# Nine of the twenty chunk states computed on ScalarE in eight pieces, two half differences on GpSimd, sums and products merged, and a new order of the whole program

## The chip, the cores and the metric

The kernel runs on one core of a Trainium2 chip. The metric is the device time of one execution in microseconds, lower is better. The core has five instruction streams that run side by side, each in its own fixed order, and wait for each other through semaphores: TensorE (PE), VectorE (DVE), ScalarE (ACT), GpSimd (POOL), and SyncE (SP), which here only issues DMAs.

## The reference

Two stages, one after the other. The first is a linear attention with a decaying state, for 4 batches, 8 heads, 768 steps and 48 channels per head; the second is a gated long convolution over 768 steps, with 384 channels.

```
# stage 1, for each batch, head, step t
y[t]  = r[t] @ (state + outer(u*k[t], v[t]))
state = w[t][:, None] * state + outer(k[t], v[t])
# stage 2, x = y with the heads side by side: [4, 768, 384]
x1, x2, x3 = split(x @ w_proj, 3)
conv = irfft(rfft(x2, axis=1) * rfft(filter, axis=0), axis=1)
out  = (x1 * conv * x3) @ w_out
```

## The kernel before

**Stage 1 by chunks.** The 768 steps of a batch are 6 chunks of 128 steps, so there are 24 chunks, numbered 0 to 23 (chunk c belongs to batch c // 6). For a chunk, SP loads w, k, r and v (`ldw`, `ldk`, `ldr`, `ldv`, line 464, 192 KB each, into rings of six tiles). ACT takes the logarithm of w (`lw`, L470). PE sums it over the steps by triangular masks (`cs`, L474, and `ce`, L480 to L486). ACT takes exponentials (`en`, `eq`, or in place in PSUM as `enp`, `eqp`). DVE or POOL multiplies them with k and r (`kh`, `khp`, `q`, `qp`). PE transposes the two products (`tqk`, L561), and a copy brings them to SBUF (`tT`, the tile qkT, on ACT by L237). PE multiplies them to 8 score matrices of 128x128 (`sc`, L574) in one PSUM tile that is two banks wide, of which there is one only. DVE masks them into SBUF (`mt`, L581). PE then makes the chunk's output y from scores and v and from the queries and the state before the chunk (`y`, L622 and L627; `yb` also adds the bonus term by a matmul with vc, L619; otherwise `xn` on DVE adds it, L639). `xc` copies an output with the bonus in it to SBUF.

**The state.** `kv` (L600, L602) adds to the old state the chunk's outer products in PSUM, 128x384; `S` (L610) scales that by the chunk's whole decay `ph`, which differs by partition and by group of 48 columns: four pairs of heads, two heads each. It is one DVE instruction in which the eight decays of a partition are spread over 48 columns each. The next chunk's `kv` and `y` read the result. The last chunk of a batch has no state, so there are 20.

**The bonus.** `rk` is r times k (POOL L535), `rku` is that times u, `cc` its sum over the channels (DVE L541), `vc` is v times that sum (POOL L555).

**Stage 2 by batches.** Each output is transposed (`yt`, `xT`); the projections `p1`, `p3` (L688) make x1 and x3, which become the gate `g`; sums and differences of the two halves of a batch in time (`sa`, `sb`, `fp`, `fm`) go through the projection `x2` (L719), and cosine and sine matrices F give the spectrum `f` (L734, L739). DVE multiplies it by the filter's spectrum T (`da`, `db`, L761, L764), `pp` adds the two products (L767), `i1` and `i2` transform back (L773), `s` and `d` are their sum and difference, `yy` multiplies by the gate (L807), `po` (L852) projects out, `o` copies, `st` stores. Batch 3, the last, does the way back in halves of the time (`i1h`, `i2h`, `ech`, `sh`, `dh`, `yyh`, `poa`, `pob`).

**The filter.** At the start ACT makes F by a sine (`sin`, L346 to L351, with two loads of its function tables beside the one of `tLn`, L342). The filter is loaded by one DMA of 1152 KB (`ldfilt`, L360); `fs` and `fd` (DVE L399, L402) make the sum and the difference of its halves, `hf` (PE L409, L416) transforms them, and `ht` (ACT L434, a copy from PSUM scaled by a column of the tile rot) and `hr` (DVE L439) turn the result into T.

**The order.** The program is one string, ORDER, of words like `A:ht0.1` or `P:hf0@2`: engine, operation, arguments, PSUM bank. `emit` issues the words one by one, so each engine's words, read in turn, are its queue. There is no scheduler at run time: an instruction that waits holds up all behind it on its engine. A POOL word that ends in `!` also waits for the last DVE instruction of certain kinds ahead of it in the string.

Of the kernel before, what the change touches and what calls it, by code (L numbers as in the profile page):

```python
# [10 lines left out]
FP32 = mybir.dt.float32  # L11
BF16 = mybir.dt.bfloat16
# [30 lines left out]
A:ht0.1 A:mc2 A:ht0.0 S:ldv1 A:enp2 P:hf1@3 P:tqk0@5 V:mem6 V:ms0 A:tT0 P:kv0@0 V:hr0.1 V:ms2
V:hr0.0 V:S0 P:hf2@2 V:khp2 P:sc0@8 A:he P:cs3@0 A:ht1.1 S:ldk3 S:ldw4 P:tqk2@1 A:ht1.0 V:rku2
G:vc0! G:v1! P:ce3@3 P:hf3@5 S:ldr3 S:ldv2 V:mt0 V:cc2 V:hr1.1 P:yb0@2 A:eq3 P:sc1@8 V:hr1.0 G:vc1!
S:ldw5 A:enp3 A:lw4 S:ldv3 V:mt1 A:tT2 A:v2 A:xc0 G:rk3! G:rku3! P:kv1@3 P:hf4@4 P:cs4@5 G:vc2! V:S1
V:khp3 A:enp4 A:ht2.0 P:yb1@1 P:yt0@2 G:v3! G:q3! P:kv2@3 S:ldk4 S:ldr4 V:cc3 S:ldr5 A:lw5 A:ht2.1
S:ldk5 G:rk4! G:vc3! P:ce4@0 P:sc2@8 P:ce5@4 A:xT0 A:xc1 A:eq5 V:S2 S:ldv4 P:hf5@3 P:tqk3@2 A:eqp4
# [904 lines left out]
```

## Time and profile before

| what | value |
|---|---|
| three timed runs | 150.94, 151.19, 152.24 us; median 151.19 |
| the profiled execution | 150.74 us, of which the span from first to last instruction is 148.9 |
| busy, of the span | PE 134.0, DVE 134.8, ACT 130.7, POOL 108.8 us |
| DMA | 27.40 MB, 184 GB/s on the mean |
| stretches, from the view by windows | 0 to 20 us: DVE busy 12.4, ACT 15.5; 20 to 130 us: DVE 109.2, ACT 104.6; 130 to 149 us: DVE 13.2, ACT 10.7 |

Busy time counts an engine as busy from the start of an instruction to its end, and two instructions in a row overlap: the next one begins before the last one has ended. What an instruction costs in a full queue is therefore the time from its start to the next one's start, called its **step** below. It is read from the view in order of time, whose first two columns are the start and the duration.

### The profile page before, as it was taken

To read this page: it belongs to the slowest core of one execution; us is meant where nothing else is said; L and a number is where in the kernel's file an instruction comes from. 1 tells how busy PE (TensorE), PEld (TensorE's weight loads), DVE (VectorE), ACT (ScalarE), POOL (GpSimd) and SP (SyncE) were. 2 spreads that over 40 slices of the span, in tenths; PEclk is the share of its full clock that TensorE was granted. 3 is DMA by queue.
4 is the path that set the end of the run, shared out by engine and by line. 5 is a ranking of instruction groups with operands and counts; after the bars stand their busy time and mean duration, and the time that the engine had idled before them with its cause. 6 is when DMAs were issued, how large, how long until landed. Compare 5 with 4: busy or idle time off the path is not lost.

```text
span 148.9 us, 4080 instructions
## 1 busy us (share of the span) xinstructions
PE 134.0 (90%) x1499; PEld 89.9 (60%) x1499; DVE 134.8 (91%) x278; ACT 130.7 (88%) x274; POOL 108.8 (73%) x133
## 2 busy tenths in 40 slices
PE   6625699898999899999999999999999999999990
PEld 6423365666655567777666757666666776555840
DVE  6534999999999999999999999999999999999950
ACT  3799699999999899999999999999999975768470
POOL 7034179995579799999659999695599995846530
PEclk9955559999999999999999999999999999999998
DMA  4998999999999999989999999989980046001854
GB/s 80 212 278 218 181 210 187 219 188 243 178 258 201 263 203 183 217 167 214 227 232 200 222 204 194 198 168 219 229 186 0 4 173 254 0 0 53 314 210 170
DMA packets 105702, 27.40 MB, mean 184 GB/s; under 512 B 100305, under 2 KB 105682, under 8 KB 105682
## 3 DMA queue, kind: packets, MB, share of 16 engines
q1 hardware_dynamic: 105682, 27.14, 81.1%
q8 instruction: 11, 0.18, 0.5%
q14 instruction: 9, 0.07, 0.1%
HBM read 22.41 MB, written 4.72 MB: 182 GB/s over the span
## 4 chain that ended last, share of the span: by engine, by line
PE 68%; DMA 12%; SPq 5%; POOL 4%; DVE 4%; issue 3%; ACT 1%; ACTq 0%; DVEq 0%; POOLq 0%
PE p L688 14%; PE po L852 8%; PE i L773 6%; PE x L719 6%; PE tqk L561 6%; DMA filt<-in_moe_filter_fft_dram 5%; SPq L464 5%; PE sc L574 4%; DMA ldv<-in_v_dram 4%; DMA ldk<-in_k_dram 3%; PE f L739 3%; PE y L627 2%; PE yt L650 2%; PE cs L474 2%; PE kv L602 2%
## 5 line engine op out<-in xcount | busy, mean ns | idle before, releaser
L535 POOL TENSOR_TENSOR rk<-ldr,ldk 128x384 bf16<-128x384 f32 x23 | 23.0, 1003 | 11.1 <-DMA ldr<-in_r_dram 5.6
L688 PE MATMUL p<-xT,wproj 128*128 128x384 bf16 x144 | 28.8, 326 | 0.0
L555 POOL TENSOR_TENSOR vc<-v,cc 128x384 bf16<-128x384 bf16 x24 | 19.9, 831 | 10.5 <-PE sc L574 3.1
L581 DVE TENSOR_TENSOR mt<-sc,mask_excl 128x1024 bf16<-128x1024 f32 x21 | 25.4, 1210 | 0.1
L237 ACT ACTIVATE qkT<-tqk 128x1024 bf16<-128x1024 bf16 x22 | 22.7, 1031 | 0.7 <-PE tqk L561 0.5
L532 POOL TENSOR_TENSOR qk<-ldr,eq 128x384 bf16<-128x384 f32 x20 | 20.1, 1007 | 3.3 <-DVE rku L538 1.8
L561 PE MATMUL tqk<-ident,qk 128*128 128x128 bf16 x192 | 16.2, 228 | 2.6 <-POOL qk L532 1.8
L688 PEld LDWEIGHTS <-wproj 128*128 128x128 bf16 x144 | 13.0, 97 | 7.4 <-ACT wproj L237 0.3
L561 PEld LDWEIGHTS <-qk 128*128 128x128 bf16 x192 | 12.7, 102 | 5.5 <-POOL qk L532 2.2
L470 ACT ACTIVATE lg<-ldw 128x384 bf16<-128x384 f32 x24 | 12.6, 532 | 2.8 <-DMA ldw<-in_w_dram 2.8
L852 PE MATMUL po<-wout,y 128*128 128x384 bf16 x72 | 14.4, 326 | 0.0
L237 ACT ACTIVATE x<-p 128x384 bf16<-128x384 f32 x24 | 11.7, 505 | 1.5 <-PE p L688 1.5
L237 ACT ACTIVATE ab<-x 128x384 bf16<-128x384 f32 x24 | 11.7, 501 | 1.1 <-PE x L719 0.8
L538 POOL TENSOR_TENSOR rku<-rk,u_bc 128x384 bf16<-128x384 bf16 x13 | 11.8, 913 | 0.4
L541 DVE TENSOR_REDUCE cc<-rku 128x8 f32<-128x384 bf16 x22 | 11.7, 537 | 0.0
L499 ACT ACTIVATE eq<-ce 128x392 f32<-128x392 f32 (+1 forms) x21 | 10.6, 514 | 0.6 <-PE ce L486 0.3
L764 DVE TENSOR_TENSOR UB<-f,T 128x768 bf16<-128x768 f32 x12 | 11.1, 943 | 0.0
L237 ACT ACTIVATE v<-ldv 128x384 bf16<-128x384 f32 x20 | 10.8, 548 | 0.3 <-DMA ldv<-in_v_dram 0.2
L237 ACT ACTIVATE xT<-yt 128x384 bf16<-128x384 bf16 x22 | 10.8, 503 | 0.2
L610 DVE TENSOR_TENSOR S<-kv,eq 128x384 bf16<-128x384 f32 x20 | 10.9, 543 | 0.0
L528 POOL TENSOR_TENSOR qk<-ldk,en 128x384 bf16<-128x384 f32 x10 | 10.0, 1003 | 0.8 <-DMA ldk<-in_k_dram 0.8
L761 DVE TENSOR_TENSOR UA<-f,T 128x768 bf16<-128x768 f32 x11 | 10.3, 943 | 0.1
(152 smaller groups left out, 372.9 us busy)
## 6 DMA issues: line engine op xcount, KB each, us to landing
ldw<-in_w_dram SPq DMA_DIRECT2D x24, 192.0 KB, 3.8
ldr<-in_r_dram SPq DMA_DIRECT2D x24, 192.0 KB, 4.2
ldk<-in_k_dram SPq DMA_DIRECT2D x24, 192.0 KB, 3.7
ldv<-in_v_dram SPq DMA_DIRECT2D x24, 192.0 KB, 3.8
out_dram<-o SPq DMA_DIRECT2D x12, 192.0 KB, 2.3
out_dram<-filt SPq DMA_DIRECT2D x12, 192.0 KB, 2.2
o<-in_moe_w_proj_dram SPq DMA_DIRECT2D x3, 576.0 KB, 6.0
filt<-in_moe_filter_fft_dram SPq DMA_DIRECT2D x1, 1152.0 KB, 8.0
```

The lines of the kernel that those rows point to most:

```text
L237: return nc.scalar.activation(out=o, in_=i, func=AF.Copy)
L470: nc.scalar.activation(out=lg_b[c % 3][:, :, 0:D], in_=ld["w"][c % LD], func=AF.Ln)
L532: return two(e).tensor_mul(qk_b[c % 3][:, 0, :, 0:D], ld["r"][c % LD], eq)
L535: return two(e).tensor_mul(rk_b[c % 2], ld["r"][c % LD], ld["k"][c % LD])
L538: return two(e).tensor_mul(rku_b[c % 2], rk_b[c % 2], u_bc)
L541: nc.vector.tensor_reduce(out=cc_b[c % 3], in_=rku_b[c % 2], axis=AX.X, op=ALU.add)
L555: return two(e).tensor_mul(vc_b[c % 3], v_b[c % 4], cc_b[c % 3].to_broadcast([L, H, D]))
L561: nc.tensor.transpose(p[:, x, j, :], qk_b[c % 3][:, x, 2 * j:2 * j + 2, :], ident)
L581: nc.vector.tensor_mul(mt_b[c % 3], bank_of[f"sc{c}"].rearrange("p q j t -> p (q j) t"), dataclasses.replace(m[:, :], ap=[m[:, :].ap[0], [ ...
L688: nc.tensor.matmul(p, wproj[:, n, cb, fb * L:(fb + 1) * L], xT_b[b % 2][:, NT * hf:NT * hf + NT, cb, :], start=(cb == 0), stop=(cb == CB - 1),
L764: nc.vector.tensor_mul(UB[:, n], twice(bank_of[f"f.{b}.{2 * n + 1}"][:, :]), t2(n, 1))
L852: nc.tensor.matmul(p, y_b[0][:, cb, ti * L:(ti + 1) * L], wout[:, cb, :], start=(cb == FIRST[0]), stop=(cb == FIRST[-1]),)
```

## The change

**States on ACT.** The states of chunks 0, 1, 4, 6, 8, 9, 10, 21 and 22 move from DVE to ACT. ACT can scale by one column of decays per instruction, so each state becomes eight instructions of 128x48.

**GpSimd.** In batch 3, two of the six half differences are made by POOL (`dgh`) from SBUF copies that ACT makes of both sides (`ich` beside `ech`); before, DVE read one side from PSUM. `fd` goes from DVE to POOL.

**Merged.** The products `yy` of a batch's three channel blocks become one instruction of 128x2304 for batches 0 to 2 (`yym`), the sums `pp` become one for batches 0, 1 and 3 (`ppm`), and `fp`, `fm` become one for both parities (`fpm`, and `fmm` for batches 0 to 2). The tiles sd, fo and SD become one tile each for that.

**Counts that shift.** On ACT: 9 states (72 instructions) more, copies `v` 20 to 15, `xc` 15 to 10, `xT` 22 to 19, `wc` 3 to 2, spectrum copies `X` 1 to 5, gate copies `gc` 6 to 8, one table load fewer. On DVE: states 20 to 11, `xn` 9 to 14, `cc` 22 to 24, products from PSUM `da` and `db` 23 to 19. On POOL: `q` 20 to 17, `rku` 13 to 10, `pp` 3 to 1, `v` 4 to 9. On PE: `yb` 15 to 10.

**The order.** All of ORDER is written anew. Two places in it follow.

SP's queue from its start (the tiles' numbers tell the chunk: ldw_79 is chunk 0, ldw_80 chunk 1, ldw_82 chunk 3). Before:

```order
L464 DMA ldw_80<-in_w_dram 128x8x48
L357 DMA u_row<-in_u_dram 1x384
L464 DMA ldw_79<-in_w_dram 128x8x48
L464 DMA ldr_91<-in_r_dram 128x8x48
L464 DMA ldk_85<-in_k_dram 128x8x48
L464 DMA ldk_86<-in_k_dram 128x8x48
L464 DMA ldw_81<-in_w_dram 128x8x48
L464 DMA ldr_92<-in_r_dram 128x8x48
L360 DMA filt<-in_moe_filter_fft_dram 128x6x384
L464 DMA ldv_97<-in_v_dram 128x8x48
L464 DMA ldw_82<-in_w_dram 128x8x48
```

and in the change:

```order
L487 DMA ldw_80<-in_w_dram 128x8x48
L487 DMA ldk_85<-in_k_dram 128x8x48
L487 DMA ldw_79<-in_w_dram 128x8x48
L487 DMA ldv_97<-in_v_dram 128x8x48
L487 DMA ldr_91<-in_r_dram 128x8x48
L487 DMA ldk_86<-in_k_dram 128x8x48
L487 DMA ldr_92<-in_r_dram 128x8x48
L487 DMA ldr_93<-in_r_dram 128x8x48
L383 DMA filt<-in_moe_filter_fft_dram 128x6x384
L487 DMA ldk_88<-in_k_dram 128x8x48
L487 DMA ldw_82<-in_w_dram 128x8x48
```

Ahead of these rows stand ldk_87, ldw_81 and u_row. The filter had seven loads of 192 KB ahead of it and now has ten; ldw_82, chunk 3's w, had nine and the filter, and now has twelve and the filter.

ACT's queue around the first copy of the filter's transform (`E<-hf,rot`, the word ht0.1). Before:

```order
L499 ACTIVATE eq_114<-ce_337 128x392
L237 ACTIVATE m_b<-mtr_318 128x2x192
L237 ACTIVATE v_121<-ldv_97 128x384
L470 ACTIVATE lg_103<-ldw_82 128x8x48
L434 ACTIVATE E_160<-hf_352,rot 128x384
L237 ACTIVATE m_b<-mtr_346 128x2x192
L434 ACTIVATE E_159<-hf_352,rot 128x384
```

and in the change, with the first state behind it:

```order
L522 ACTIVATE eq_113<-ce_334 128x392
L529 ACTIVATE cs_359<-cs_359 128x384
L493 ACTIVATE lg_103<-ldw_82 128x8x48
L457 ACTIVATE E_158<-hf_381,rot 128x384
L457 ACTIVATE E_157<-hf_381,rot 128x384
L240 ACTIVATE qkT_133<-tqk_361 128x1024
L648 ACTIVATE S_137<-kv_370,eq_112 128x48 x8
L533 ACTIVATE ce_404<-ce_404 128x384
```

In both, the first copy stands right behind the logarithm of chunk 3's w (`lg_103<-ldw_82`); in the change less of ACT's other work stands ahead of the two. The state of chunk 0 is eight instructions, each of which scales by one column of the tile eq.

The diff, without most of ORDER and without the renaming of tiles:

```diff
 ORDER = """
-V:mem1 V:mem3 G:mkd! G:mke! G:iota! V:mem0 A:tLn G:mki! S:ldw1 S:ldu S:ldw0 A:lw1 V:mem4 V:mem2
+A:tS0 S:ldk2 S:ldw2 G:iota0! G:mki! G:mkd! G:hm0! V:mem7 V:mem5 G:mke! S:ldu S:ldw1 S:ldk0 S:ldw0
...
     def op_S(e, c):
         ph = eq_b[c % 3][:, C:].rearrange("p (a b) -> p a b", b=2)
+        if e == "A":
+            for j in range(HP):
+                for i in (0, 1):
+                    nc.scalar.activation(
+                        out=S_b[nth(c)][:, j, i], in_=bank_of[f"kv{c}"][:, j, i], func=AF.Copy,
+                        scale=ph[:, j, i:i + 1],
+                    )
+            return
         nc.vector.tensor_mul(
             S_b[nth(c)], bank_of[f"kv{c}"], ph.to_broadcast([L, HP, 2, D])
         )
...
+    def op_fpm(e, b):
+        return two(e).tensor_add(fo[:, :, 0], sd[:, :, 0], sd[:, :, 2])
+
+    def op_fmm(e, b):
+        return two(e).tensor_sub(fo[:, :, 1], sd[:, :, 0], sd[:, :, 2])
...
+    def op_ppm(e, b):
+        return two(e).tensor_add(P_b[b % 2], UA, UB)
+
...
+    def op_ich(e, b, cb, a):
+        copy(e, I_b[cb][:, QUART * a:QUART * a + QUART], bank_of[f"i1h.{b}.{cb}.{a}"][:, 0:QUART])
+
...
+    def op_dgh(e, b, cb, a):
+        sl = slice(QUART * a, QUART * a + QUART)
+        return nc.gpsimd.tensor_sub(back(SD[:, cb, :], a, 1), I_b[cb][:, sl], E_b[cb][:, sl])
+
...
+    def op_yym(e, b):
+        return two(e).tensor_mul(y_b[0], SD, g_b[b % 2])
```

More of the change, by code (lines that the diff above doesn't have):

```diff
@@ L43 @@
[L43 to L48, printed above, removed]
@@ new lines @@
+G:v1! G:vc0! P:cs3@0 A:eqp3 V:mem6 G:v2! P:mtr2@4 A:ms2 S:ldr3 P:hf2@1 G:rk3! S:ldw5 S:ldv3 S:ldk4
+V:mc2 P:tqk1@2 A:en3 A:lw4 V:hb0 V:rku3 V:he A:ht1.1 A:tT1 S:ldr4 P:hf3@4 P:yb0@0 A:ht1.0 A:ph3
+G:kh3! V:cc3 P:kv1@2 G:v3! P:cs4@5 V:qp3 G:vc1! A:lw5 S:ldv4 S:ldw6 S:ldr5 S:ldw8 A:en4 A:S1 P:ce4@1
+V:hr1.1 A:xc0 G:kh4! A:eq4 S:ldk5 P:sc1@8 A:hb1 G:q4! V:mt1 P:tqk3@3 A:tT3 P:hf4@5 V:hr1.0 P:sc2@8
+P:yt0@1 P:kv2@0 P:cs5@4 G:vc3! G:vc2! P:yb1@2 P:ce5@3 A:enp5 A:lw6 A:eqp5 A:xc1 V:mt2 V:S2 P:sc3@8
+P:tqk4@0 V:mt3 P:y3@2 V:qp5 G:rk4! A:tT4 V:khp5 A:ht2.0 P:kv3@0 A:xT0 A:lw8 P:yb2@3 S:ldv5 S:ldk6
@@ new lines @@
+P:po1.4@5 P:p33.1.0@4 P:p13.1.0@3 G:pp2.2! P:sc23@8 P:kv22@1 P:y21@2 A:gc3.1.0 A:gc3.2.0 P:f2.0@0
+V:cc23 V:cc22 A:x13.1.0 V:mt23 A:v23 V:xn21 V:da2.0 P:po1.3@3 G:vc23! A:S22 P:po1.0@4 P:y23@2
+P:p13.2.0@1 P:yt21@0 A:o1.0 A:o1.4 V:xn23 A:x13.2.0 P:p13.0.0@4 G:vc22! P:y22@2 V:pp2.0 P:yt23@1
+A:x13.0.0 A:xT21 V:pp2.1 V:gm2.2.1 G:sb21! A:o1.3 V:xn22 V:sa23 V:sa21 V:sb23 P:i22.2@5 P:i22.1@4
+P:yt22@3 V:sb22 A:ec2.2 V:fpm3 V:fm3.0 P:i12.1@2 P:i22.0@5 A:xT22 P:x23.1.1@0 P:i12.0@3 A:ec2.1
+A:ec2.0 P:i12.2@4 P:x23.1.0@5 V:xT23 V:fm3.1 V:d2.1 V:gm2.1.1 V:d2.0 V:d2.2 A:ab3.1.1 V:s2.1
@@ new lines @@
+A:ab3.1.0 P:x23.0.2@0 P:x23.1.2@1 G:sa22! A:ab3.0.2 P:x23.0.1@5 A:ab3.0.1 A:ab3.1.2 P:p13.2.1@0
+S:st1.4 P:x23.0.0@2 A:ab3.0.0 V:s2.2 P:p13.1.1@5 G:gm3.2.0! P:f3.5@1 P:f3.0@2 V:gm3.1.0 V:s2.0
+A:x13.1.1 A:X3.0 A:X3.5 A:x13.2.1 P:f3.1@3 P:f3.2@5 P:f3.3@2 V:gm2.0.1 V:yym2 P:p13.0.1@1 P:f3.4@0
+G:ua3.0! P:po2.1@4 V:db3.0 V:da3.1 V:ub3.2 P:po2.3@5 P:po2.4@3 A:X3.4 S:st1.3 A:X3.3 S:st0.1 S:st1.2
+S:st0.4 S:st1.1 V:ua3.2 V:ub3.1 A:o2.4 A:o2.3 A:o2.1 A:x13.0.1 P:p33.2.1@2 P:po2.0@0 P:po2.2@3
+V:ppm3 P:p33.1.1@5 S:st0.0 V:g3.1.1 A:gc3.2.1 P:i2h3.0.0@1 A:o2.2 P:i2h3.1.0@4 V:gm3.2.1
@@ L177 @@
     xT_b = ring("xT", 2, [L, NCH, CB, L], BF16)
-    sd_b = ring("sd", 2, [L, NT, CB, L], BF16)
+    sd = consts.tile([L, 2, NT, CB, L], BF16)
     x1_b = ring("x1", 1, [L, CB, S], BF16)
     g_b = ring("g", 2, [L, CB, S], BF16)
-    fo_b = ring("fo", 2, [L, 2, CB, L], BF16)
+    fo = consts.tile([L, 2, 2, CB, L], BF16)
     ab_b = ring("ab", 1, [L, 2, NT, C], BF16)
@@ L187 @@
     E_b = ring("E", 3, [L, HALF], FP32)
-    SD_b = ring("SD", 3, [L, S], BF16)
+    I_b = ring("I", 3, [L, HALF], FP32)
+    SD = consts.tile([L, CB, S], BF16)
     y_b = ring("y", 1, [L, CB, S], BF16)
@@ L194 @@
     u_bc = consts.tile([L, H, D], BF16)
+    hm = consts.tile([L, CB, H], BF16)
+    uh = consts.tile([L, CB, H], BF16)
     filt = consts.tile([L, NCH, C], FP32)
@@ L325, in op_uv, with op_hm, op_um, op_uw @@
         copy(e, u_bc.rearrange("p h d -> p (h d)"), bank_of["us"])
+    def op_hm(e, k_):
+        nc.gpsimd.memset(hm, 1.0)
+        for lo, m in ((0, 1), (D - 1, -1)):
+            nc.gpsimd.affine_select(
+                out=hm, in_=hm, pattern=[[m * L, CB], [-m * D, H]], base=lo,
+                channel_multiplier=m, compare_op=ALU.is_ge, fill=0.0,
+            )
+    def op_um(e, k_, bank):
+        p = ps("um", bank, (L, CB, H))
+        for cb in range(CB):
+            nc.tensor.matmul(
+                p[:, cb, :], u_top[:, cb * L:(cb + 1) * L], mask_incl[:, 0:H],
+                start=True, stop=True,
+            )
+    def op_uw(e, k_):
+        nc.vector.tensor_mul(uh, bank_of["um"], hm)
     def op_ang(e, ti):
@@ L333, in op_ang, with op_tS, op_sn, op_sr @@
             )
-    def op_angn(e, k_):
-        d = ang.rearrange("p (n s) -> p n s", s=S)[:, :, HALF]
         two(e).tensor_scalar(
-            out=d, in0=tcol, scalar1=float(HALF), scalar2=0.5 * UNIT, op0=ALU.mult, op1=ALU.add,
-        )
+            out=ang[:, ti * S + HALF:ti * S + HALF + 1], in0=tcol[:, ti:ti + 1],
+            scalar1=float(HALF), scalar2=0.5 * UNIT, op0=ALU.mult, op1=ALU.add,
+        )
+    def op_tS(e, k_):
+        nc.scalar.preload_act_table(AF.Sin)
     def op_tLn(e, k_):
         nc.scalar.preload_act_table_set("natural_log_exp_and_others")
-    def op_sin(e, k_):
-        for ti in range(NT):
-            nc.scalar.activation(
-                out=F[:, ti, :], in_=low[:, ti * S:(ti + 1) * S], func=AF.Sin,
-                scale=TWO_PI / UNIT,
-            )
+    def op_sn(e, ti):
+        nc.scalar.activation(
+            out=F[:, ti, :], in_=low[:, ti * S:(ti + 1) * S], func=AF.Sin,
+            scale=TWO_PI / UNIT,
+        )
+    def op_sr(e, k_):
         nc.scalar.activation(out=rot, in_=rang, func=AF.Sin, scale=TWO_PI / (2 * S))
-        nc.scalar.preload_act_table_set("natural_log_exp_and_others")
     def op_rsc(e, k_):
@@ L541, in op_cc, with op_rt, op_rT, op_cu @@
         nc.vector.tensor_reduce(out=cc_b[c % 3], in_=rku_b[c % 2], axis=AX.X, op=ALU.add)
-    def op_rh(e, c):
-        x = rku_b[c % 2]
-        return two(e).tensor_add(rh_b[c % 2], x[:, :, 0:D // 2], x[:, :, D // 2:])
-    def op_ch(e, c):
-        nc.vector.tensor_reduce(out=cc_b[c % 3], in_=rh_b[c % 2], axis=AX.X, op=ALU.add)
+    def op_rt(e, c, bank):
+        p = ps(f"rt{c}", bank, (L, CB, L), BF16)
+        f = rk_b[c % 2].rearrange("p h d -> p (h d)")
+        for cb in range(CB):
+            nc.tensor.transpose(p[:, cb, :], f[:, cb * L:(cb + 1) * L], ident)
+    def op_rT(e, c):
+        copy(e, rT_b[c % 2], bank_of[f"rt{c}"])
+    def op_cu(e, c, bank):
+        p = ps(f"cu{c}", bank, (L, H))
+        for cb in range(CB):
+            nc.tensor.matmul(
+                p, rT_b[c % 2][:, cb, :], uh[:, cb, :], start=(cb == 0), stop=(cb == CB - 1)
+            )
+    def op_cv(e, c):
+        copy(e, cc_b[c % 3], bank_of[f"cu{c}"])
     def op_v(e, c):
@@ L645, in op_xc, with op_xr, op_xg @@
         copy(e, xn_b[c % 3], bank_of[f"y{c}"].rearrange("p h d -> p (h d)"))
+    def op_xr(e, c):
+        op_xc(e, c)
+    def op_xg(e, c):
+        x = xn_b[c % 3]
+        return two(e).tensor_add(x, x, vc_b[c % 3].rearrange("p h d -> p (h d)"))
     def op_yt(e, c, bank):
@@ L706, in op_g, with op_gg @@
         )
+    def op_gg(e, b, fb, hf):
+        nc.vector.tensor_mul(
+            g_b[b % 2][:, fb, halves[hf]], bank_of[f"p3.{b}.{fb}.{hf}"],
+            bank_of[f"p1.{b}.{fb}.{hf}"],
+        )
     def op_gc(e, b, fb, hf):
@@ L806, in op_yy @@
     def op_yy(e, b, cb):
-        return two(e).tensor_mul(y_b[0][:, cb, :], SD_b[cb], g_b[b % 2][:, cb, :])
+        return two(e).tensor_mul(y_b[0][:, cb, :], SD[:, cb, :], g_b[b % 2][:, cb, :])
     def half(name, bank, b, cb, a, slots):
@@ L841, in op_dh, with back, op_ic, op_dg @@
         )
+    def back(x, a, n):
+        o = x[:, HALF * a + QUART:HALF * a + HALF]
+        return dataclasses.replace(
+            o, offset=o.offset + (QUART - 1) * o.ap[-1][0],
+            ap=[o.ap[0]] + ([[HALF * o.ap[-1][0], n]] if n > 1 else []) + [[-o.ap[-1][0], QUART]],
+        )
+    def op_ic(e, b, cb):
+        copy(e, I_b[cb], bank_of[f"i1.{b}.{cb}"])
+    def op_ich(e, b, cb, a):
+        copy(e, I_b[cb][:, QUART * a:QUART * a + QUART], bank_of[f"i1h.{b}.{cb}.{a}"][:, 0:QUART])
+    def op_dg(e, b, cb):
+        i1, i2 = (x[cb].rearrange("p (a t) -> p a t", a=2) for x in (I_b, E_b))
+        return nc.gpsimd.tensor_sub(back(SD[:, cb, :], 0, 2), i1, i2)
+    def op_dgh(e, b, cb, a):
+        sl = slice(QUART * a, QUART * a + QUART)
+        return nc.gpsimd.tensor_sub(back(SD[:, cb, :], a, 1), I_b[cb][:, sl], E_b[cb][:, sl])
     def op_yyh(e, b, cb, a):
         sl = halves[a]
-        return two(e).tensor_mul(y_b[0][:, cb, sl], SD_b[cb][:, sl], g_b[b % 2][:, cb, sl])
+        return two(e).tensor_mul(y_b[0][:, cb, sl], SD[:, cb, sl], g_b[b % 2][:, cb, sl])
+    def op_yym(e, b):
+        return two(e).tensor_mul(y_b[0], SD, g_b[b % 2])
+    def op_yyq(e, b, cb, a, pt):
+        sl = slice(HALF * a + QUART * pt, HALF * a + QUART * pt + QUART)
+        return two(e).tensor_mul(y_b[0][:, cb, sl], SD[:, cb, sl], g_b[b % 2][:, cb, sl])
     FIRST = (2, 0, 1)
```

182 lines of the change are left out of this document (86 added, 96 removed).

## The prediction

> **What bounds the kernel now.** First the view by windows, over three stretches that I cut at events found below. Its columns are the length, then busy us of PE, PE's weight loads, DVE, ACT and POOL (instructions in brackets), clock, DMA share and GB/s.
>
> ```profile
> 17.40:117.20 99.80, 97.27 (x1195) 65.78 (x1193) 98.87 (x190) 97.68 (x208) 84.07 (x94) 0.98 0.95 197
> 119.40:144.50 25.10, 25.10 (x218) 16.32 (x217) 23.81 (x53) 16.98 (x41) 16.44 (x17) 1.00 0.38 138
> 117.20:148.90 31.70, 27.65 (x242) 17.69 (x234) 26.01 (x56) 20.17 (x47) 18.57 (x19) 0.98 0.38 138
> ```
>
> From 17.4 to 117.2 us PE, DVE and ACT are all busy over 97%: no engine has room for much more. ACT is idle for 2.1 us there, POOL for 15.7. From 119.4 PE alone is without a gap, and ACT is idle a third of the time. So the end is PE's queue behind `sc` of the last chunk, and the question is when that one starts.
>
> Next the view in order of time, at the start:
>
> ```profile
> 2.85 2.07 SPq L464 DMA_DIRECT2D ldk<-in_k_dram  x2
> 6.81 0.63 SPq L360 DMA_DIRECT2D filt<-in_moe_filter_fft_dram  x1
> 6.92 0.56 DVE L535 TENSOR_TENSOR rk<-ldr,ldk 128x384 bf16<-128x384 f32 x1 [1.68 <-DMA ldk<-in_k_dram]
> 9.71 1.00 POOL L535 TENSOR_TENSOR rk<-ldr,ldk 128x384 bf16<-128x384 f32 x1 [5.62 <-DMA ldr<-in_r_dram]
> 14.80 1.36 DVE L399 TENSOR_TENSOR UA<-filt 128x1152 bf16<-128x1152 f32 x1 [2.00 <-DMA filt<-in_moe_filter_fft_dram]
> 16.20 0.52 ACT L470 ACTIVATE lg<-ldw 128x384 bf16<-128x384 f32 x1 [0.28 <-DMA ldw<-in_w_dram]
> 16.22 2.10 PE L416 MATMUL hf<-UA,F 128*128 128x384 bf16 x6 [1.28 <-DVE UA L399]
> 17.40 0.58 ACT L434 ACTIVATE E<-hf,rot 128x384 f32<-128x384 f32 x1 [0.67 <-PE hf L416]
> ```
>
> The start is paced by DMA. DVE waits for the first k (fourth load in SP's queue) until 6.92, POOL for the second r (seventh) until 9.71: 2.79 us for three loads, 0.93 each, and SP too needs 2.07 us to issue two. The filter stands behind those seven and ends DVE's wait at 14.80. From it runs `fs`, then `hf`, then ACT's first copy at 17.40, 2.60 us after the landing. ACT's rows stand in one queue, so that copy holds up everything behind it.
>
> **The filter is later.** The change puts ten loads ahead of the filter where seven were: three times 0.93 is 2.8 us, so `fs` starts at 17.6 and ht0.1 at 20.2. The same three loads more stand ahead of chunk 3's w, which lands at 19.0 instead of 16.2, with 0.8 us to spare for its logarithm. The other way, SP's issues: the filter is the twelfth, at the pace of 0.93 from the fifth at 2.85 it goes out at about 9.4, 2.6 later than at 6.81. Bounds 2.3 to 3.1; I take **2.8**. DVE has little to do meanwhile: by steps, 7.9 us of its work stand ahead of `fs` now, 6.6 before.
>
> **A state on ACT.** No row shows a piece of 48 columns; these bound it (ACT's rows alone, in order of time):
>
> ```profile
> 25.72 0.58 ACT L434 ACTIVATE E<-hf,rot 128x384 f32<-128x384 f32 x1
> 26.18 0.53 ACT L470 ACTIVATE lg<-ldw 128x384 bf16<-128x384 f32 x1
> 26.59 0.59 ACT L434 ACTIVATE E<-hf,rot 128x384 f32<-128x384 f32 x1
> 27.05 0.51 ACT L237 ACTIVATE xT<-yt 128x384 bf16<-128x384 bf16 x1
> 27.43 0.52 ACT L237 ACTIVATE xn<-y 128x384 bf16<-128x384 f32 x1
> 28.57 1.07 ACT L237 ACTIVATE qkT<-tqk 128x1024 bf16<-128x1024 bf16 x1
> 29.48 0.55 ACT L506 ACTIVATE cs<-cs 128x384 f32<-128x384 f32 x1
> 32.77 0.17 ACT L513 ACTIVATE eq<-ce 128x8 f32<-128x8 f32 x1
> 32.83 1.02 ACT L237 ACTIVATE qkT<-tqk 128x1024 bf16<-128x1024 bf16 x1
> ```
>
> A step of 384 columns from PSUM is 0.38 us (27.05 to 27.43), one of 8 columns 0.06 (32.77 to 32.83): 0.85 ns a column, so 48 columns are 0.09. The copy that scales by a column of a tile, as the pieces do, steps 0.46 (25.72 to 26.18), 0.08 more than the plain one. So 0.17 by steps; without the charge for the column 0.09; with no overlap at all, from the duration 0.17 of 8 columns, 0.03 and 0.08, it is 0.28. I take 0.19, near the steps, as the eight wait for nothing between them, a little above because the row of 8 columns is a single one. **A state is then 1.5 us on ACT**, 0.75 to 2.3 by the ends.
>
> The Trainium skill (ScalarE: Activation LUTs, What ACT_TABLE_LOAD costs) has 186 ns plus 0.833 ns per column, 93 ns more for each operand that is a column, and an overlap of 93 between neighbours. The slope and the charge agree with 0.85 and 0.08 here. By it a piece would be an estimated 226 ns and a state 1.8, and the sum below 2.3 us higher.
>
> **ACT from ht0.1 to tT23,** the last chunk's copy of `tqk`:
>
> ```profile
> 24.52 0.52 ACT L237 ACTIVATE v<-ldv 128x384 bf16<-128x384 f32 x1
> 24.94 0.49 ACT L237 ACTIVATE xn<-y 128x384 bf16<-128x384 f32 x1
> 20.13 0.51 ACT L237 ACTIVATE T<-T 128x384 bf16<-128x384 bf16 x1
> 20.68 0.48 ACT L456 ACTIVATE T<-hf 1x384 bf16<-1x384 f32 x1
> 21.06 1.02 ACT L434 ACTIVATE E<-hf,rot 128x384 f32<-128x384 f32 x2
> L237 ACT ACTIVATE wproj<-o 128x1152 bf16<-128x1152 f32 x2 | 2.3, 1170 | 0.2 <-DMA o<-in_moe_w_proj_dram 0.2
> ```
>
> Counted in ORDER, that stretch gains eight states (12.2 us). It loses three `v` at a step of 0.42 (1.3), five `xc`, one `xT` and one `x1` against one `X` more at 0.38 (2.3), one weight copy of 1.17 with its 0.1 of overlap (1.1), one exponential (0.4), and `he`, 20.13 to 21.06 (0.9). It gains one `tT` at 0.91 (28.57 to 29.48), and two `ms` for two `mc` (0.1). That is 6.0 out and 1.0 in, so **the net is 12.2 - 4.9 = +7.3 us**.
>
> How much of it does idle time swallow? By busy time ACT has 2.1 us. By steps it has more: the 206 words of the stretch, 23 of 1024 columns at 0.91, 37 `lw` and `v` and 16 in-place exponentials at 0.42, 117 of 384 columns at 0.37 to 0.38, three weight copies at 1.06, six scaled ones at 0.46, and the rest 1.8, come to 94 of its 99.8, 5.8 spare. A queue that is always late loses little to waits, but still something wherever a first operand comes just in time; I take 4.0 of the 7.3 as swallowed, bounds 2.1 and 5.8.
>
> **The end.** Around the last `sc`:
>
> ```profile
> 117.16 1.07 ACT L237 ACTIVATE qkT<-tqk 128x1024 bf16<-128x1024 bf16 x1
> 118.46 0.65 PE L852 MATMUL po<-wout,y 128*128 128x384 bf16 x3
> 118.95 0.33 PE L600 MATMUL kv<-S,ident 128*128 128x384 bf16 x1
> 119.38 0.40 PE L574 MATMUL sc<-qkT 48*128 48x128 bf16 x8
> 142.53 1.69 PE po L852 x9
> 144.63 0.48 ACT filt L237
> ```
>
> tT23 ends at 118.2, its `sc` starts at 119.4: 1.2 us that ACT may be late for nothing. Behind that `sc`, PE has two more `po`, one `kv`, but one `p1` and three `p3` less; three matmuls of such a group step 0.49 (118.46 to 118.95), the `kv` 0.43 (118.95 to 119.38): two groups less and one `kv` more are 0.6 us less. PE's last `po` and the way out (144.6 to 148.9) stay.
>
> **Sum** for the profiled execution (150.74; its span 148.9 and 1.84 around it): 2.8 + 7.3 - 4.0 - 1.2 - 0.6 = +4.3, 155.0 us. The median of the three runs, 151.19, lies 0.45 above that execution, so I forecast **155.5**. With pieces of 0.17 and all 5.8 spare swallowed: +1.4. With pieces of 0.28 and 2.1: +12.
>
> **The edits that cost nothing there,** and their covers.
>
> ```profile
> 118.77 0.94 DVE L761 TENSOR_TENSOR UA<-f,T 128x768 bf16<-128x768 f32 x1
> 119.63 0.54 DVE L610 TENSOR_TENSOR S<-kv,eq 128x384 bf16<-128x384 f32 x1
> 120.10 1.21 DVE L581 TENSOR_TENSOR mt<-sc,mask_excl 128x1024 bf16<-128x1024 f32 x1
> L807 DVE TENSOR_TENSOR y<-SD,g 128x768 bf16<-128x768 bf16 x9 | 4.7, 549 | 0.1
> L845 DVE TENSOR_TENSOR y<-SD,g 128x384 bf16<-128x384 bf16 x3 | 1.2, 404 | 0.1
> L535 POOL TENSOR_TENSOR rk<-ldr,ldk 128x384 bf16<-128x384 f32 x23 | 23.0, 1003 | 11.1 <-DMA ldr<-in_r_dram 5.6 <-DVE sgn L315 5.5
> L546 POOL TENSOR_TENSOR rh<-rku 128x192 f32<-128x192 bf16 x2 | 1.1, 549 | 0.0
> ```
>
> *DVE* gives away nine states at a step of 0.47 (119.63 to 120.10; 4.2), four products from PSUM at 0.86 (118.77 to 119.63; 3.5) and `fd` (1.3). It takes five `xn` (2.3), three `cc` for two `ch` (0.9), three products of SBUF copies (1.4), and some small ones (2.2 net). Merging: from 384 to 768 columns the duration grows from 0.40 to 0.55, so most of a step is not a fixed part; six instructions of 2304 columns, bounded by three single ones above and by the columns alone below, change it by 0.4 at most either way. Behind `fs` DVE has 1.8 us less. That is not paid out, because DVE waits for `sc`, and that for ACT.
>
> *POOL* makes `fd` in 3.0 us (three times 1.00) in place of DVE's 1.36. It is done at 17.6 + 1.3 + 3.0 = 21.9; ACT reaches ht1.1 about 5 us behind ht0.1, at 25, so 1.6 us cover it after `hf2`. The two half differences take 0.55 each there, and the copies for them ACT's idle third; uncovered they would cost 0.5 each. PE's five `yb` less give 0.8 us where PE is not the last to arrive.
>
> **Rivals.**
>
> *The column is free (0.16).* If a piece steps 0.09, eight states are 6.0, the net on ACT 1.1, and its spare time takes that. Then DVE and PE set the pace as now: `fs` is 2.8 late, and 1.8 less stands behind it: +1.0, 152.2. For it: the pieces wait for nothing. Against: 0.46 against 0.38 above.
>
> *DVE's gain comes through (0.08).* If pieces are cheap and also the filter comes by the time that DVE reaches `fs`, say because the first loads flow better, the delay is gone and DVE's 1.8 us are left: 149.4, faster. It decides where `fs` starts no later than 15. Against: the 0.93 us a load, twice (6.92, 9.71).
>
> *States late for their readers (0.14).* A state of 1.5 us stands in ACT's queue behind other work, and `kv` and `y` of the next chunk wait for it on PE, in order, with all behind them. Chunks 8, 9, 10 follow each other: if each hands on 1.5 - 0.47 = 1.0 us, 3 us come on top: 158.5. For it: PE is busy 97%. Against: the next `kv` stands an average chunk, some 4 us, later.
>
> *The sum above (0.62).*
>
> **Chances.** A measurement of this kernel tells about 1% (1.5 us) from no change. The sum and the late states give slower, 0.76; the free column lies within 1%, 0.16; faster 0.08. The range 151.8 to 160.0 takes in the late states and most of the free column's case; the likeliest case alone has 152.6 (the +1.4 above) to 159; what lies from there to +12 needs pieces without any overlap, which the steps speak against.
>
> **What would show it.** Right: `fs` waits for the filter until 17 to 18 and ht0.1 starts near 20; the pieces follow each other at 0.17 to 0.23; ACT is busy 99% from 20 to 120, DVE less than 97% there and waiting for PE's `sc`, and that for qkT; the last `sc` starts near 124. Wrong: ACT idle over 3 us in that stretch, `fs` at or before 15.5, or pieces at 0.1.

## The result, and the profile after

The changed kernel takes 157.87 us (median of 4 runs, 156.89 to 158.05) where the kernel before takes 151.56 (four runs beside these; the three known to the prediction had 151.19): 1.040 times as long, 95% interval 1.0335 to 1.0469. It is slower, as forecast (155.5, range 151.8 to 160.0).

The profiled execution took 156.89 us with a span of 155.2, 6.3 more than the span before. The page's busy time:

```profile
PE 134.3 (87%) x1497; PEld 89.8 (58%) x1497; DVE 136.7 (88%) x274; ACT 136.9 (88%) x337; POOL 103.1 (66%) x130
```

ACT has 6.2 us more work, 136.9 for 130.7, and the span is 6.3 longer: its time outside work did not change, 18.3 us for 18.2. DVE's grew from 14.1 to 18.5, though its work grew too, from 134.8 to 136.7. So DVE, the busiest engine before, now waits more, and ACT is as busy as it is. The view by windows, over the stretch from ht0.1 to tT23, and over the one from the last `sc` to the end (columns as in the prediction):

```profile
18.95:124.40 105.45, 97.93 (x1194) 65.86 (x1193) 101.44 (x179) 103.90 (x260) 84.80 (x95) 0.99 0.88 183
125.80:155.20 29.40, 25.26 (x215) 16.04 (x214) 23.10 (x53) 20.64 (x57) 8.35 (x9) 0.99 0.40 142
```

ACT is busy for 103.90 of 105.45 us, DVE for 96%, PE for 93%. Before, DVE had 99% and PE 97%. The end after the last `sc` is as long as it was. Inside the long stretch the full engine changes:

```profile
60.00:80.00 20.00, 18.29 (x247) 12.95 (x244) 18.15 (x37) 19.75 (x57) 15.25 (x18) 1.00 0.97 201
80.00:100.00 20.00, 20.00 (x241) 13.34 (x239) 20.00 (x32) 19.23 (x41) 17.45 (x20) 1.00 1.01 198
```

From 60 to 80 us, where three of the nine states lie, ACT is the full one; from 80 to 100, where there is none of the nine, PE and DVE are without a gap, as they were before.

The start in the view in order of time (start, length, engine, line, what, and in brackets the idle time before it), first SP's and DVE's rows of the filter, then ACT's:

```profile
9.19 0.83 SPq L383 DMA_DIRECT2D filt<-in_moe_filter_fft_dram  x1
...
16.36 1.36 DVE L422 TENSOR_TENSOR UA<-filt 128x1152 bf16<-128x1152 f32 x1 [0.27 <-DMA filt<-in_moe_filter_fft_dram]
```

```profile
17.73 0.52 ACT L493 ACTIVATE lg<-ldw 128x384 bf16<-128x384 f32 x1 [0.88 <-DMA ldw<-in_w_dram]
18.95 1.05 ACT L457 ACTIVATE E<-hf,rot 128x384 f32<-128x384 f32 x2 [0.70 <-PE hf L439]
...
20.80 1.65 ACT L648 ACTIVATE S<-kv,eq 128x48 bf16<-128x48 f32 x8
22.27 0.57 ACT L533 ACTIVATE ce<-ce 128x384 f32<-128x384 f32 x1
```

The sum of the filter starts 1.56 us later than before (16.36 for 14.80), and ht0.1 1.55 later (18.95 for 17.40). The first state takes ACT from 20.80 to 22.27: 1.47 us, 0.184 a piece. Around chunks 8 and 9, ACT and then DVE:

```profile
61.71 0.48 ACT L533 ACTIVATE ce<-ce 128x384 f32<-128x384 f32 x1
62.12 1.63 ACT L648 ACTIVATE S<-kv,eq 128x48 bf16<-128x48 f32 x8
63.58 0.55 ACT L240 ACTIVATE xT<-yt 128x384 bf16<-128x384 bf16 x1
...
65.10 1.73 ACT L648 ACTIVATE S<-kv,eq 128x48 bf16<-128x48 f32 x8
66.57 1.18 ACT L240 ACTIVATE qkT<-tqk 128x1024 bf16<-128x1024 bf16 x1
```

```profile
65.61 0.54 DVE L564 TENSOR_REDUCE cc<-rku 128x8 f32<-128x384 bf16 x1
67.53 0.69 DVE L241 COPY qkT<-tqk 128x1024 bf16<-128x1024 bf16 x1 [1.38 <-PE tqk L596]
...
68.60 1.22 DVE L616 TENSOR_TENSOR mt<-sc,mask_excl 128x1024 bf16<-128x1024 f32 x1
```

ACT goes from one instruction to the next without a gap, while DVE stands 1.38 us for `tqk`. PE in turn waits for the states, whose `kv` occupies a PSUM bank until ACT has read it; the list of waits (us in total, times, longest) has

```profile
PE tqk L596 <- ACT S L648: 1.3, 2, 0.8
PE p L744 <- ACT S L648: 1.2, 2, 0.7
PE hf L432 <- ACT S L648: 1.0, 1, 1.0
```

### The profile page after: what moved, and what is told of

It is laid out like the page before. It is cut to its first block, busy times and chain, and to the rows that moved or that the text cites. A ratio compares the mean times of both kernels' runs of the same rounds, so it can differ in the third digit from the quotient of the medians.

```text
span 155.2 us, 4127 instructions
## 1 busy us (share of the span) xinstructions
PE 134.3 (87%) x1497; PEld 89.8 (58%) x1497; DVE 136.7 (88%) x274; ACT 136.9 (88%) x337; POOL 103.1 (66%) x130
## 4 chain that ended last, share of the span: by engine, by line
PE 43%; ACT 18%; DVE 1%; issue 1%; ACTq 0%
PE p L744 10%; PE po L945 6%; PE x L781 6%; ACT S L648 5%; PE i L838 4%; PE tqk L596 3%; ACT qkT L240 2%; PE sc L609 2%; PE f L801 2%; PE yt L700 1%; ACT en L515 1%; PE y L670 1%; ACT xT L240 1%; ACT eq L522 1%; PE f L796 1%; PE cs L497 1%
## 5 line engine op out<-in xcount | busy, mean ns | idle before, releaser
L744 PE MATMUL p<-xT,wproj 128*128 128x384 bf16 x144 | 29.9, 326 | 1.2 <-ACT S L648 1.2
L564 DVE TENSOR_REDUCE cc<-rku 128x8 f32<-128x384 bf16 x24 | 12.7, 542 | 6.4 <-POOL rku L561 6.4
L555 POOL TENSOR_TENSOR qk<-ldr,eq 128x384 bf16<-128x384 f32 x17 | 17.0, 1002 | 1.7 <-ACT eq L522 1.7
L648 ACT ACTIVATE S<-kv,eq 128x48 bf16<-128x48 f32 x72 | 15.2, 372 | 0.0
L493 ACT ACTIVATE lg<-ldw 128x384 bf16<-128x384 f32 x24 | 13.9, 585 | 0.9 <-DMA ldw<-in_w_dram 0.9
L551 POOL TENSOR_TENSOR qk<-ldk,en 128x384 bf16<-128x384 f32 x11 | 11.0, 999 | 3.7 <-ACT en L515 2.3
L838 PE MATMUL i<-m_b,P 128*128 128x384 bf16 x54 | 10.8, 326 | 0.0
L609 PE MATMUL sc<-qkT 48*128 48x128 bf16 x192 | 9.7, 222 | 1.1 <-DVE mt L616 1.1
L609 PEld LDWEIGHTS <-qkT 48*128 48x128 bf16 x192 | 5.7, 95 | 6.5 <-issue 4.0
L760 DVE TENSOR_TENSOR g<-p,x 128x384 bf16<-128x384 f32 x16 | 8.8, 548 | 0.8 <-PE p L744 0.8
```

The lines of the kernel that those rows point to most:

```text
L493: nc.scalar.activation(out=lg_b[c % 3][:, :, 0:D], in_=ld["w"][c % LD], func=AF.Ln)
L555: return two(e).tensor_mul(qk_b[c % 3][:, 0, :, 0:D], ld["r"][c % LD], eq)
L609: nc.tensor.matmul(p[:, par, j, :], t[p0:p0 + D, 1, j, :], t[p0:p0 + D, 0, j, :], start=True, stop=True,)
L648: nc.scalar.activation(out=S_b[nth(c)][:, j, i], in_=bank_of[f"kv{c}"][:, j, i], func=AF.Copy, scale=ph[:, j, i:i + 1],)
L744: nc.tensor.matmul(p, wproj[:, n, cb, fb * L:(fb + 1) * L], xT_b[b % 2][:, NT * hf:NT * hf + NT, cb, :], start=(cb == 0), stop=(cb == CB - 1),
L838: nc.tensor.matmul(p, P_b[b % 2][:, s // 2, s % 2, cb * L:(cb + 1) * L], m_b[:, s].rearrange("p a t -> p (a t)"), start=(i == 0), stop=(i ...
```

## The experiments

Two theories said slower in the prediction. **Load:** ACT's queue is full, so each us of states is a us of time. **Latency:** the states come late to the matmuls that read them. A third, **start**, would put the loss on the filter behind three more loads. Each ratio below is to the kernel before as it ran beside that experiment (medians 150.67 to 151.02), so ratios compare runs more closely than the times do.

**All nine states back on DVE,** at the same places of the order:

```diff
-... A:S0 ... A:S22
+... V:S0 ... V:S22
```

> The changed kernel with its nine ACT states given back to DVE, each at the same place of the order, as one instruction; all else as changed. Load theory (ACT's queue is full, the states' 1.47 us each make the rest late): ACT loses eight states, 11.7 us, in the stretch that sets the end, DVE gains 4.2 us and becomes the bound: 152.5 to 154.5 us. Start theory (the filter behind three more loads and the new order of the start are what costs, the states fit in): 156.5 to 158. Latency theory (not ACT's load, but states that come late to the matmuls that read them): 152.5 to 154.5 as well, so this run does not tell it from the load theory.

157.68 us, 1.045 of before (1.0383 to 1.0521): as slow as the change. The load theory's number was wrong, and the time lies where the start theory had put it; the run with a constant scale, below, has the same late start and is not slow. The page's busy time of the run shows what the load theory had left out, and the view by windows says the same for the middle of the run:

```profile
PE 135.5 (87%) x1497; PEld 89.6 (58%) x1497; DVE 140.7 (90%) x283; ACT 125.2 (80%) x265; POOL 102.8 (66%) x130
```

```profile
20.00:125.00 105.00, 99.21 (x1198) 65.99 (x1193) 104.00 (x185) 93.93 (x196) 83.50 (x95) 0.98 0.87 181
```

Now DVE is the full one, 104.0 of 105 us. This kernel and the one before both make all 20 states on DVE, and DVE is busy 140.7 us where it was 134.8: the rest of the change (five `xn` more, `rku`, `xT`, copies) adds 5.9 us to it.

**The states twice:** DVE makes them, ACT makes the same pieces into a tile that nobody reads.

```diff
-V:S0
+V:S0 A:Sx0
```

> As the run with the states on DVE, and ACT still makes the same eight pieces for the nine chunks at the same places, into a tile that nothing reads. So ACT's load is that of the changed kernel, and the readers get their state from DVE early. Load theory: as the changed kernel, 157 to 159 us. Latency theory: as the run with the states on DVE alone, 152.5 to 154.5. Start theory: 157 to 159.

169.61 us, 1.123 (1.1149 to 1.1317), and no theory had that. Its list of ACT's waits says why it tells nothing of the two:

```profile
ACT Sx L648 <- DVE S L663: 8.2, 6, 2.7
```

Both read the same PSUM tile, and ACT's pieces waited 8.2 us, in six places, for DVE's instruction, with ACT's whole queue behind them.

**A constant as the scale** of the 72 pieces:

```diff
-scale=ph[:, j, i:i + 1],
+scale=1e-6,
```

> The changed kernel with a constant as the scale of the 72 pieces in place of a column of decays: the decay of nine states is left out. A piece then steps about 0.09 us instead of 0.183, a state 0.75 instead of 1.47. Load theory: 0.7 us for each of eight states, 5.8 us off ACT's stretch, part of it taken by DVE and PE that become the bound: 152.5 to 154.5 us. Latency theory: each state 0.7 us earlier, of the seven with close readers some 1 to 3 us: 155 to 157. Start theory: 157 to 159.

151.84 us, 1.007 (1.0035 to 1.0102). ACT's rows of it:

```profile
60.90 0.91 ACT L648 ACTIVATE S<-kv 128x48 bf16<-128x48 f32 x8
61.62 0.57 ACT L240 ACTIVATE xT<-yt 128x384 bf16<-128x384 bf16 x1
```

Eight pieces in 0.72 us, 0.09 each in place of 0.184. That is 9 times 0.75, 6.7 us less on ACT, and the time falls by most of that: 6.0 by the medians, 5.0 by the two ratios. The filter's sum starts at 16.95, no earlier than in the change, so start is not the main cause; latency expected a fall of 1 to 3.

**The same with filler behind each state,** so that the state is early and the queue full:

```diff
+        nc.scalar.activation(out=Sx, in_=warm, func=AF.Copy)
+        nc.scalar.activation(out=Sx[:, 0:L], in_=warm[:, 0:L], func=AF.Copy)
```

(a word `A:fill0` behind `A:S0`, and so on).

> The kernel with a constant scale (decay of nine states left out), and behind each of those states two copies on ACT, of 512 and 128 columns, from a constant tile into one that nothing reads: about 0.7 us per state, as much as the column of decays cost. The state is early for its readers, ACT's queue is as full as in the changed kernel. Load theory: 156.5 to 159 us, as the changed kernel. Latency theory (what cost was the state's late arrival at its readers): 151.5 to 153.5, as with the constant scale alone.

157.83 us, 1.050 (1.0437 to 1.0567), the time of the change. ACT's rows in order of time, and the page's busy time:

```profile
62.46 0.91 ACT L653 ACTIVATE S<-kv 128x48 bf16<-128x48 f32 x8
63.18 0.70 ACT L645 ACTIVATE Sx<-warm 128x512 bf16<-128x512 bf16 x1
63.91 0.31 ACT L646 ACTIVATE Sx<-warm 128x128 bf16<-128x128 bf16 x1
64.13 0.47 ACT L241 ACTIVATE xT<-yt 128x384 bf16<-128x384 bf16 x1
```

```profile
PE 133.9 (86%) x1497; PEld 89.6 (58%) x1497; DVE 136.9 (88%) x274; ACT 137.6 (88%) x355; POOL 103.2 (66%) x130
```

ACT goes on from the state at 63.18, after 0.72 us, and the filler takes the place of the column's cost. It is somewhat longer than meant: 0.95 us (63.18 to 64.13) for the column's 0.75, 1.6 us more over eight states. PE's listed waits for a state on ACT fall from 4.0 us in the change to 0.4, and others, for what stands behind the filler, take their place. By the medians the time is the change's, by the ratios 1.0% above it. So work that nobody reads costs about what the column did: it is load. The lateness of the states, their banks included, has at most the 1.6 us by which the filler is too long, and by the ratios nothing.

**Four pieces of 96 columns,** by the decay of the first head of each pair (the second head's is left out):

```diff
-                for i in (0, 1):
-                    nc.scalar.activation(
-                        out=S_b[nth(c)][:, j, i], in_=bank_of[f"kv{c}"][:, j, i], func=AF.Copy,
-                        scale=ph[:, j, i:i + 1],
-                    )
+                nc.scalar.activation(
+                    out=S_b[nth(c)][:, j], in_=bank_of[f"kv{c}"][:, j], func=AF.Copy,
+                    scale=ph[:, j, 0:1],
+                )
```

> The changed kernel with each ACT state in four pieces of 96 columns, each by the decay of its first head alone (the second head's own decay is left out). By the steps of the changed kernel's trace (0.183 us for 48 columns, 0.83 ns a column more) a piece is 0.22 and a state 0.9 us instead of 1.47: 5.1 us off ACT in all, 4.6 of it ahead of the last score copy. Load theory: 152.5 to 154 us, between the eight pieces at 157.9 and the plain scale at 151.8. If what costs is the number of columns or the waiting for the state as such: over 156.

152.32 us, 1.012 (1.0065 to 1.0177). ACT's rows and the page's busy time:

```profile
61.10 1.02 ACT L647 ACTIVATE S<-kv,eq 128x96 bf16<-128x96 f32 x4
61.99 0.52 ACT L240 ACTIVATE xT<-yt 128x384 bf16<-128x384 bf16 x1
```

```profile
PE 132.9 (88%) x1497; PEld 88.9 (59%) x1497; DVE 136.2 (90%) x274; ACT 131.6 (87%) x301; POOL 102.8 (68%) x130
```

0.89 us a state, 0.22 a piece, as reckoned; as many columns are read, each piece still scales by a column, and only the number of pieces halves.

**The kernel before with the nine states on ACT,** old order:

> The kernel before with the same nine states on ACT in pieces, each at the same place of its old order; nothing else changed. Load theory: ACT gets 11.7 us more in the stretch to the last score copy, and about 3 of it fall into idle time, 1 into slack at the end: 157.5 to 161 us. Latency theory: the same sign, 153 to 156. Start theory (the states fit in): 151 to 152.5.

168.52 us, 1.116 (1.1078 to 1.1238). Its page's busy time:

```profile
PE 139.2 (83%) x1499; PEld 92.5 (55%) x1499; DVE 132.6 (79%) x269; ACT 144.3 (86%) x346; POOL 108.5 (65%) x133
```

The sign is that of load and of latency alike, and the size is neither's. ACT works 13.6 us more, and beyond that stands 4.6 us longer (span 167.1 less 144.3 is 22.8, for 18.2 before). By busy time none of the work fell into idle time, and in an order made for states on DVE, waits came on top. Which waits, and why, was not tried.

**Four of the nine back on DVE** (chunks 6, 8, 9, 10):

> The changed kernel with four of its nine ACT states (chunks 6, 8, 9, 10) back on DVE. With all nine on ACT or all nine on DVE the time was the same, 157.9 and 157.7, so two full queues are suspected: ACT in the one, DVE in the other. Two bounds: ACT loses 5.9 us, DVE gains 1.9, both then lie below what they had: 153 to 155.5. One common cause outside the states (start, PE, new order): 157 to 158.5 again.

157.25 us, 1.047 (1.0398 to 1.0545): splitting the states between the two engines gains nothing. The mask `mt` is made once for each chunk; us between its starts for chunks 0, 5, 12 and 23, in the views in order of time, show where each kernel loses:

| kernel | mt0 to mt5 | mt5 to mt12 | mt12 to mt23 | mt23 to the end |
|---|---|---|---|---|
| constant scale | 14.7 | 40.0 | 45.2 | 28.2 |
| the change | 15.3 | 43.4 | 45.9 | 28.9 |
| nine on DVE | 16.0 | 42.8 | 45.6 | 29.5 |
| four on DVE | 15.8 | 42.9 | 45.7 | 28.9 |

The rows of the masks of chunks 0, 5 and 12 in the run with four on DVE:

```profile
22.53 1.21 DVE L616 TENSOR_TENSOR mt<-sc,mask_excl 128x1024 bf16<-128x1024 f32 x1
...
38.36 1.21 DVE L616 TENSOR_TENSOR mt<-sc,mask_excl 128x1024 bf16<-128x1024 f32 x1
...
81.26 1.21 DVE L616 TENSOR_TENSOR mt<-sc,mask_excl 128x1024 bf16<-128x1024 f32 x1
```

Each row of the table is one execution, and the first stretch shows how far to trust it: the change and the run with four on DVE do the same work there and differ by 0.5. Only the middle stretch (chunks 6, 8, 9, 10) differs by clearly more, and there it hardly matters where the four states stand. With the constant scale DVE and PE are both without a gap from 55 to 80 us (busy 25.00 of 25.00), so states there cost time on DVE as well as on ACT. Four states at 0.47 are 1.9 of the 2.9 us between 40.0 and 42.9; where the other 1.0 comes from was not traced. A bound is not the larger of two sums over the whole program; it can change from stretch to stretch.

**The filter late in the kernel before,** three loads moved ahead of it:

```diff
-S:ldfilt S:ldv0 S:ldw3 ... S:ldr2
+S:ldv0 S:ldw3 ... S:ldr2 S:ldfilt
```

> The kernel before with its filter load moved behind three more loads (v of chunk 0, w of chunk 3, r of chunk 2), so that ten stand ahead of it as in the changed kernel; nothing else changed. In the changed kernel the sum of the filter started 1.56 us later than before. If DVE is the bound from there on, as its row without gaps says, all of it shows: 152.3 to 154 us. If the start is hidden by later idle time: 150.5 to 151.8.

152.54 us, 1.018 (1.0085 to 1.0267). The filter's first sum, in order of time:

```profile
17.34 1.36 DVE L399 TENSOR_TENSOR UA<-filt 128x1152 bf16<-128x1152 f32 x1 [4.24 <-DMA filt<-in_moe_filter_fft_dram]
```

`fs` is 2.54 us late, 0.85 a load, and the last mask 2.0: most of a late start arrives at the end. So a late filter costs about 1.6 us here; for the 1.56 by which it is late in the change, that in proportion is an estimated 1.0 of the 6.3.

**The merged sums and products alone** in the kernel before:

> The kernel before with the merged sums and products alone: one instruction for both parities of fp (batches 0 to 2) and fm (0 and 2), one for the three channel blocks of yy (0 to 2), one for pp of batch 1; old order, all else as before. DVE saves about 0.07 us for each pair and 0.14 for each third, 0.9 us in all. If DVE is the bound: 150.0 to 150.6. If what the merging holds back (the first matmul waits for a longer instruction) takes it again: 150.7 to 151.7.

151.33 us, 1.002 (0.9973 to 1.0069): no difference that can be told, either way.

**The filter early in the kernel before.** First with the load itself moved up in the string:

> The kernel before with its filter load one place earlier in SP's queue (ahead of r of chunk 1), and with the work that waits for that r (rk, rku, cc, tqk, the copy qkT of chunk 1) and v and w of chunks 0 and 3 moved behind the first use of the filter on their engines. One load is 0.93 us. If DVE is the bound from the filter on, the opposite of the late filter's +1.65: 149.9 to 150.7 us. If chunk 1, now late, holds up the queues instead: 151 to 152.5.

159.05 us, 1.057 (1.0512 to 1.0627). This run does not answer its question. The filter's tile first serves as scratch for the angles of F, and the load now stood ahead of two of the three angle computations that read it, so these waited for the load and used its numbers. Then with the load in its old place and r of chunk 1 behind it:

```diff
-S:ldr1 ... S:ldfilt
+S:ldfilt S:ldr1
-G:rk1! G:kh0! ... V:rku1 V:cc0 V:cc1 V:fs ... A:v0 A:lw3 A:ht0.1 A:mc2 A:ht0.0
+G:kh0! G:rk1! ... V:cc0 V:fs ... A:ht0.1 A:mc2 A:ht0.0 A:v0 A:lw3 ... V:hr0.0 V:rku1 V:cc1
```

(each engine's words alone; `tqk1` and `tT1` move behind `kv0`).

> The early filter in the kernel before once more, with the order of the string kept where it decides what is computed: the load of the filter stays where it was in the string and r of chunk 1 goes behind it, so that the filter has six loads ahead of it; work that waits for that r stands behind the first use of the filter, chunk 0's transposes ahead of chunk 1's. Nothing of the computation is left out. If DVE is the bound from the filter on: 149.9 to 150.7 us (0.93 us, or some part of it). If chunk 1, now late, holds up the queues instead: 151 to 153.

152.89 us, 1.010 (1.006 to 1.0138): 1% slower, where 150.7 or less was hoped for. DVE's rows of the filter's sum and of the first mask:

```profile
13.40 1.36 DVE L1414 TENSOR_TENSOR UA<-filt 128x1152 bf16<-128x1152 f32 x1 [3.83 <-DMA filt<-in_moe_filter_fft_dram]
...
23.30 1.23 DVE L1596 TENSOR_TENSOR mt<-sc,mask_excl 128x1024 bf16<-128x1024 f32 x1 [1.09 <-PE sc L1589]
```

`fs` comes 1.4 us earlier and the first mask 2.1 later than before (23.30 for 21.17): the new order that the earlier filter needs costs more than it brings. Which part of that order costs it was not taken apart. No kernel here beat the one before.

## Why the prediction was right

**Which engine, and which way: right.** ACT is busy for 98.5% of its stretch, DVE for 96% and PE less, and the constant scale, the four pieces and the filler together show that ACT's load is the main cause.

**The price of a state: right.** 1.47 us measured, 1.5 forecast, from two steps and the charge for the column that the trace of before showed. The constant scale and the four pieces confirm both parts: 0.09 without the column, 0.22 with 96 columns. The Trainium skill (ScalarE: Activation LUTs, What ACT_TABLE_LOAD costs) gave an estimated 0.226 for the piece; the measurement, 0.184, decides, and its charge of 93 ns per column operand agrees (0.184 less 0.09).

**The start: the right step, too large.** 2.8 us forecast, 1.55 measured. The filter went out at 9.19, as reckoned (9.4), but its sum started 7.2 us after that instead of the 8.0 of before; why is not shown. In the kernel before, three loads more cost 2.54. The start of the sum at 16.36 lies between the prediction's own signs, 17 to 18 for right and 15.5 for wrong.

**What idle time swallows: the term that was off.** The stretch was to grow by 7.3 - 4.0 = 3.3 us and grew by 5.65, from 99.8 to 105.45. With eight states at 1.47, and the forecast's 4.9 taken as it stands, the net is 11.8 - 4.9 = 6.9, of which 6.9 - 5.65 = 1.2 was swallowed, where the forecast had 4.0 and a lower bound of 2.1; by busy time ACT's idle time fell only from 2.1 to 1.55. The 5.8 us "spare by steps" (4.4 to 5.6 when the same steps are added up again) were not spare. A likely reason, not tested: they are places where an instruction begins a little later than it could, because its input comes just then, and such places come back behind every delay. The row of busy time was the better guide.

**The slack and the end: small errors.** tT23 starts 7.21 us later (124.37 for 117.16), `sc` 6.47 (125.85 for 119.38), so 0.74 of the slack of 1.2 was used. Behind it the end is 0.2 us shorter, not 0.6. The sum as measured: 1.55 + 5.65 - 0.74 - 0.17 = 6.3, the growth of the span, where the forecast had 4.3. That it came this near is partly luck: the start was taken 1.25 too large, the stretch 2.35 too small. (The low case, "+1.4", comes to +1.2 by its own terms.)

**An edit taken as free: right, for another reason.** `fd` on POOL took 2.63 us (3.0 forecast) and ended at 20.4 us. `hf2`, which reads it, started at 22.51 and had waited 0.96 for the first state to be read from the bank that it needs, not for `fd`.

**The rivals.** That a free column would give 152.2 was the nearest number of all: with the constant scale it is 151.84, and DVE is the bound (busy 104.6 of 105 us from 20 to 125). But the number came out by luck: its 2.8 for the start was 2.15 there (16.95 for 14.80), and where it had 1.8 less work on DVE, DVE was busy for 1.3 more (136.1 for 134.8 over the whole span). The late states are not the main mechanism (filler run). That DVE's gain comes through could not happen, as there was no gain.

**What was overlooked: DVE got no relief.** The prediction had DVE give away 9.0 us and take 6.8, 2.2 less in all. Its busy time grew by 1.9, from 134.8 to 136.7, and by 5.9 with the nine states back on it, where the same items without the states' 4.2 come to 2.0. What was taken too small is what DVE takes over; among it, in the groups by shape:

```profile
L555 DVE TENSOR_TENSOR qk<-ldr,eq 128x384 bf16<-128x384 f32 x3 | 2.2, 772 | 0.0
L241 DVE CAST wproj<-o 128x1152 bf16<-128x1152 f32 x1 | 0.9, 911 | 0.0
```

The first of these groups had one instruction before, the second none. With ACT as the bound this touched the forecast of the time little, but it is why the states back on DVE, which fill it, are as slow as on ACT.

## What to carry to other kernels

Before moving work off a full engine, price it on the engine that takes it, by its steps: the nine states are 4.2 us on DVE and 13.2 on ACT, since ACT takes one instruction and one column charge for each group of 48 columns. Then count again what the rest of the edit puts on the engine that is to be relieved. When several queues are over 97% busy, count hardly any idle time as a place to put work into (here 1.2 of 6.9 us), and look at each stretch by itself. Putting filler in place of a suspected cost, with the result itself early, tells load from latency, if the filler is as long as the cost.

## What the runs showed of the hardware

A copy on ACT that scales by a column of a tile steps 0.184 us for 48 columns from PSUM, while each lasts 0.29 to 0.48 (ns, shortest, median and longest, in the view by tile of the changed kernel):

```profile
L648 ACT ACTIVATE S<-kv,eq x72: 288/354/477, 20.8 to 128.5; 128x48 bf16<-128x48 f32 x72
```

So neighbours overlap by about half of their length. Merging saves little on DVE, as its groups by shape show (products and sums of SBUF tiles):

```profile
L934 DVE TENSOR_TENSOR y<-SD,g 128x2304 bf16<-128x2304 bf16 x3 | 4.1, 1350 | 0.0
...
L829 DVE TENSOR_TENSOR P<-UA,UB 128x768 bf16<-128x768 bf16 x2 | 1.0, 548 | 0.0
```

Three instructions of 768 columns at 0.548 last 1.64 us and one of 2304 lasts 1.35, 0.15 less for each instruction saved; in the kernel before, the merging alone made no difference that can be told (1.002).
